# A forward Fourier transform in quarters instead of halves, an earlier table for the square root, and a new order of work, in a routed attention and gated long convolution on one core

## The chip, the cores and the metric

The kernel runs on one core of one Trainium2 chip. The metric is device time in microseconds (us) of one execution. The engines are TensorE (PE, its weight loads PEld), VectorE (DVE), ScalarE (ACT), GpSimd (POOL) and SyncE (SP), which here only issues transfers.

## What is computed

Two layers in a row, for B = 4 batches, H = 8 heads, S = 768 positions, D = 64 columns a head and 16 clusters; the model width is H x D = 512:

```
q_assign = argmax(q_n @ c_n.T);  k_assign = argmax(k_n @ c_n.T)        # nearest centroid of each q and k
scores = where(q_assign == k_assign, q @ k.T / 8, -1e9)
x = softmax(scores) @ v                                                 # [4, 768, 512]
x1, x2, x3 = split(x @ w_proj, 3)
x2_conv = irfft(rfft(x2, axis=1) * rfft(filter_fft, axis=0), axis=1)    # circular convolution along the positions
out = (x1 * x2_conv * x3) @ w_out
```

## The kernel before

**Stages.** Eight groups of four heads (n = 0 to 7, two a batch), each in two pairs of heads (pr). `routing(n)` transposes q and k on PE, compares them with the centroids, takes the arg max on DVE, and puts the result as 16 extra rows into the operands of the scores (`aug`), so that the mask comes out of the score matmul itself. `attention(n, pr)` does the scores of 128 keys at a time (line 658, by `product`), the exponential on ScalarE into `p` (667, 670), p times v on PE in float32 (681), and the sums of p on DVE (695, tile `acc`); the denominators go through transfers that fold `acc` (729, issued by POOL) and come back as `rb`; line 775 divides and stores `xT`. Every second group `hyena(b)` follows for the batch that is complete, woven into the attention of the next ones; the last batch's stands alone at the end.

**hyena(b).** U (line 807) computes x2 in six matmul groups of 64 + 64 positions. A DFT over 768 positions is done in halves: position t and its mirror image are added and subtracted (820, tile `uv2`), so that even and odd frequencies each need a sum over 384 terms, three tiles of 128 (m = 0 to 2). `spectrum(ps, i, cs)` (444) multiplies with the cosine (cs = 0) and sine (cs = 1) tables `fw`: for i = 0, 1 three steps each, for i = 2 (the 128 frequencies left over, half even, half odd) three pairs. A step of `product` is one matmul over all 128 rows or two side by side over 64 each (lines 71 and 73). The spectra are multiplied with the filter's (831, tile `tm`; `hm` holds the filter's spectrum) and combined into `y` (835). Then for each quarter dt of the channels: G projects x1 and x3 (861; copied at 868, multiplied at 871), I is the inverse transform (already in four parts, 878), 896 and 906 fold its parts into positions (`yy`), 909 forms `y2`, and W (919) multiplies by w_out; 929 copies and 936 stores the result.

**Setup.** `centroids` (306) loads and normalises the centroids: a square root on ScalarE (314), whose function table is loaded just before it, then six small DVE operations (`newton`, 316), a transpose on PE (325). `angles` (336) forms the tables `fw` in three rounds m of four DVE operations and two sines. `tables` (374) makes the inverse's tables from `fw` by transposes (392, 395), and the filter's spectrum: four loads of 384 KB, a sum and a difference on DVE (417), the same `spectrum`, and hm (437).

**The order.** Nothing runs in the order of the source. Each `op` gives its engines with a planned duration, a due time, what it reads and writes and which PSUM banks it takes; `Plan.place` (112) simulates the engines, always takes the ready operation with the earliest due time, chooses the engine where several are allowed, and yields the order in which all instructions are issued. Every engine then works through its instructions in that order and waits at each for what it needs. The due times come from T0, TAU1, TAU2 (247), from w0 and w1 of `hyena` (786), and from NUDGE (40), a list of corrections by number of operation. `lock=True` marks DVE and POOL operations that the plan does not let overlap. The first q and k loads (`load_qk`, 290) may go to SP or ACT; POOL issues the folding transfers in its own order.

Of the kernel before, what the change touches and what calls it, by code (L numbers as in the profile page):

```python
# [35 lines left out]
LEAD = 1.97516  # L36
FIRST = 2
BUSY = 8.32578
HELD = 4
NUDGE = {10:3.7,75:-1.5,90:7.4,91:7.4,129:-0.8,140:0.4,156:6.6,187:-5.6,193:0.1,212:-0.2,216:15.5,218:8.0,222:-3.8,243:1.1,253:-4.1,255:-7.1,256:-7.1,257:-3.0,264:4.3,274:2.3,281:0.9,288:9.1,289:11.6,328:-9.2,363:0.5,370:2.2,378:0.5,379:0.7,400:-0.2,406:1.5,409:-4.8,434:0.6,440:-3.7,479:0.8,480:-0.3,481:-1.3,494:-0.6,495:-4.2,508:-1.9,511:-0.2,518:-5.0,524:0.5,526:2.1,539:-2.3,554:10.5,568:1.6,573:0.4,587:-4.9,590:0.2,597:-2.4,617:0.7,620:-1.0,658:0.8,664:0.1,684:2.2,690:-8.8,740:1.0,759:0.5,767:0.4,779:-0.7,782:1.7,788:0.7,790:0.8,826:-0.5,828:-0.3,848:-2.2,872:-1.3,883:-5.3,888:-3.6,897:-0.8,898:-1.1,901:-3.5,915:-3.1,941:0.4,947:-0.4,969:-0.8,996:2.0,997:2.0,1026:2.7,1029:-2.1,1039:2.0,1043:-1.2,1048:1.2,1056:10.8,1062:0.4,1066:0.9,1098:-1.0,1101:0.3,1118:-2.2,1127:1.5,1130:-1.5,1143:-2.6,1194:-0.9,1255:0.7,1257:0.7,1263:0.3,1270:-0.2,1271:-1.1,1276:-3.6,1295:4.9,1317:-2.0,1321:0.4,1351:5.6,1373:-1.5,1441:9.4,1450:3.5,1461:2.0,1478:-1.3,1501:-8.3,1546:0.2,1557:0.1,1563:-0.6,1624:2.8,1630:-1.5,1634:0.3,1640:-4.0,1641:-4.0,1642:-13.7,1643:-4.0,1655:-4.1,1666:0.5,1685:-2.9,1771:-3.3,1776:0.2,1788:-7.8,1797:0.1,1808:-0.1,1809:-0.1,1827:-0.7,1841:-1.3,1844:0.9,1862:-0.4,1863:2.1,1887:2.4,1890:3.2,1898:-7.4,1901:-0.8,1902:-1.5,1903:-0.8,1904:-0.8,1905:-1.8,1906:-1.8}  # L40
# [27 lines left out]
def product(T, out, lhsT, rhs, start, stop):  # L68

    if T.whole:  # L70
        return T.nc.tensor.matmul(out, lhsT, rhs, start=start, stop=stop)  # L71
    for i in range(2):
        T.nc.tensor.matmul(out[64 * i:64 * i + 64], lhsT[:, 64 * i:64 * i + 64], rhs, start=start, stop=stop)  # L73


class Plan:
# [35 lines left out]
    def place(self, free0, banks_for, switch=0.1, wait=0.1, rate=215e3, bonus=11.03330, margin=0.02203, shape=1.60501):  # L112
# [130 lines left out]
def build(T):  # L243
# [3 lines left out]
    T0 = 20.36576  # L247
    TAU1 = 2.98452
    TAU2 = 3.43320
# [56 lines left out]
    def centroids():  # L306
# [3 lines left out]
        V = lambda: T.nc.vector  # L310
        op(("DVE", .23), lambda e: V().tensor_tensor(cen.c2, cen.c, cen.c, op=Alu.mult), 2.1, r=["c"], w=["c2"])
        op(("DVE", .22), lambda e: V().tensor_reduce(cen.ss, cen.c2, axis=AX, op=Alu.add), 2.2, r=["c2"], w=["ss"])
        op(("DVE", .15), lambda e: V().tensor_scalar(cen.ss, cen.ss, 1e-30, None, op0=Alu.max), 2.3, r=["ss"], w=["ss"])
        sq = op(("ACT", 1.5), lambda e: T.nc.scalar.activation(cen.s0, cen.ss, Act.Sqrt), 2.4, r=["ss"], w=["s0"])
# [21 lines left out]
    def angles(sq):  # L336
# [3 lines left out]
        for m in range(3):  # L340
            lo = 256 * (m // 2)
            n, r = (lambda x=x, m=m, lo=lo: x()[m % 2][:, :, lo:lo + 192] for x in (lambda: T.tm, lambda: T.ob))
            nk, rk = ("tm", m % 2, "a", m), ("ob", m % 2, "a", m)
# [13 lines left out]
            sins.append(op(("ACT", .52), lambda e, m=m, n=n: A_()(T.fw[:, :, m, 192:], n(), Act.Sin, scale=sc),  # L357
# [7 lines left out]
        op(("POOL", .2), one, 14, w=[("fw", m, 0) for m in range(3)])  # L365
# [8 lines left out]
    def tables(got):  # L374

        FW = [("fw", m, cs) for m in range(3) for cs in range(2)]
        fv = lambda: T.filt.rearrange("(w p m e) d -> w e p m d", w=2, p=64, m=3, e=2)
        for w_ in range(2):
            for e_ in range(2):
                op(("SP", .7), lambda e, w_=w_, e_=e_: T.nc.sync.dma_start(  # L380
                    T.f[w_][64 * e_:64 * e_ + 64], fv()[w_, e_]), 16.0, w=[("f", w_, e_)], byts=393e3, kind="load", after=got)
        for j in range(6):
            h = Bank("head")
            due = 20.0 + 2 * j

            def tr(e, j=j, h=h):
                tp = ap(h).bitcast(BF16)
                for m in range(3):
                    cols = (0, 192, 0, 192, 128, 320)[j]
                    o = tp[:, m * 128:(m + 1) * 128]  # L390
                    if j < 4:
                        T.nc.tensor.transpose(o, T.fw[:, j // 2, m, cols:cols + 128], T.identb)
                    else:
                        for i in range(2):
                            T.nc.tensor.transpose(o[64 * i:64 * i + 64], T.fw[:, i, m, cols:cols + 64], T.identb)
            op(("PE", .3 if j < 4 else .5), tr, due, r=FW + ["identb"], w=[h], alloc=h)
            half = lambda h, lo, hi: ap(h).bitcast(BF16)[lo:hi, :HS].rearrange("p (m c) -> p m c", c=64)[:, :, :32]
            if j < 4:
                op({"ACT": .35, "DVE": .3}, lambda e, j=j, h=h: copy(e, T.inv[:, j // 2, j % 2, 0], half(h, 0, 128)),
                   due + 1, r=[h], w=[("inv", j)], free=[h])  # L400
            else:
                for i in range(2):
                    op({"ACT": .35, "DVE": .3}, lambda e, i=i, j=j, h=h: copy(
                        e, T.inv[64 * i:64 * i + 64, i, j % 2, 1], half(h, 64 * i, 64 * i + 64)),
                       due + 1, r=[h, "inv0"], w=[("inv", j, i)], free=[h])
# [8 lines left out]
        F = [("f", a, b) for a in range(2) for b in range(2)]  # L414
        U2 = [("uv2", e, m) for e in range(2) for m in range(3)]
        for s_, o_ in ((0, Alu.add), (1, Alu.subtract)):
            op(("DVE", 1.75), lambda e, s_=s_, o_=o_: T.nc.vector.tensor_tensor(
                T.uv2[:, s_], T.f[0], T.f[1], op=o_), 30, r=F, w=U2[3 * s_:3 * s_ + 3], lock=True)
        for i in range(3):
            hs = [Bank("head"), Bank("head")]  # L420
            due = 34 + 4.0 * i
            for cs in range(2):
                op(("PE", .648), lambda e, i=i, cs=cs, h=hs[cs]: spectrum(ap(h), i, cs), due + 2 * cs, r=U2 + FW, w=[hs[cs]],
# [19 lines left out]

    def spectrum(ps, i, cs):
        for m in range(3):
            if i < 2:
                columns(ps, T.fw[:, i, m, 192 * cs:192 * cs + 128], T.uv2[:, i, m], m == 0, m == 2)
            else:
                for e in range(2):
                    T.nc.tensor.matmul(ps[64 * e:64 * e + 64], T.fw[:, e, m, 192 * cs + 128:192 * cs + 192],  # L450
                                       T.uv2[:, e, m], start=(m == 0), stop=(m == 2))
# [84 lines left out]
    def routing(n):  # L536
# [5 lines left out]
        for u in range(8):  # L542
# [7 lines left out]
            if n > 1 and ch == 0:  # L550
# [6 lines left out]
                for c in range(2):  # L557
                    op(EV384, lambda e, z=z, c=c, h=h: copy(e, T.qkT[z][:, c], bank(h.ids[c])[:, :384]), due + .9,
                       r=[h], w=[("qkT", z, c)], free=[h])
            elif n < 2:  # L560
# [6 lines left out]
                op(EV384 if n != 1 else {"ACT": .48}, lambda e, z=z, ch=ch, h=h: copy(e, T.qkT[z][:, ch], ap(h)[:, :384]),  # L567
# [10 lines left out]
        b0 = end - 24.00965  # L578
# [204 lines left out]
    def hyena(b):  # L783
        xs = b % 2
        last = b == B - 1
        w0 = A(24 * (b + 1)) + 11.85069
        w1 = A(24 * (b + 2)) + 50.52404 if b < B - 2 else A(96) + 34.73131
        if last:
            w0 = A(96) - 8.47659
# [8 lines left out]
        for m in range(3):  # L798
            for w_ in range(2):
# [374 lines left out]
```

The softmax here doesn't subtract the row's maximum and nothing guards it: scores larger than these inputs give would overflow.

## Time and profile before

| What | Value |
|---|---|
| median of 13 runs | 390.32 us (389.12 to 391.87) |
| the profiled execution's own time | 391.21 us |
| its span in the profile | 389.4 us |
| granted TensorE clock | 1.00 |
| MATMUL records that use uv2 and fw | 165: 15 over all rows, 150 in halves |
| DMA | 47.17 MB, mean 121 GB/s |

The page of the profile gives the busy time of each engine, the chain of waits that ended last, and groups of instructions by line: busy time and mean of one, then the idle time of the engine just before them and what ended it. A line number is one of the kernel, often of a helper: 71 and 73 are all products of PE, 260 and 262 all copies. The times of single instructions, counted from the span's start, come from the timeline; a stretch's busy times from the windows.

### The profile page before, as it was taken

What the parts mean: (1) busy time and instruction counts of PE and PEld (TensorE: products, weight loads), DVE (VectorE), ACT (ScalarE), POOL (GpSimd) and SP (SyncE); (2) the same over time, 40 slices, a digit from 0 to 9 for tenths busy, and PEclk for the clock granted to TensorE, in tenths of its full rate; (3) what the DMA queues carried; (4) which work ended last, traced back from release to release, by engine and by line L of the source; (5) the groups of instructions that cost most, each with busy time, mean ns of one, the idle gap of its engine ahead of it and who ended that gap; (6) DMA issues with size and microseconds to landing.
All of it is one profiled execution on the core that took longest, in us unless ns stands there. A gap on an engine that the chain in (4) does not pass through costs nothing.

```text
span 389.4 us, 8482 instructions
## 1 busy us (share of the span) xinstructions
PE 369.3 (95%) x3256; PEld 214.6 (55%) x3256; DVE 359.2 (92%) x509; ACT 269.9 (69%) x514; POOL 46.7 (12%) x92
## 2 busy tenths in 40 slices
PE   2999998999999999999999999999999999999995
PEld 1564454444455555555455554655454566558893
DVE  8898998898899999999899999999999999999782
ACT  5898687887884878787865976778865567632342
POOL 8502000000020011001010100101010100000400
PEclk9999999999999999999999999999999999999999
DMA  9819973740679759866997696855645651110214
GB/s 177 204 48 211 215 166 89 164 113 18 165 143 144 144 94 153 114 142 77 165 136 195 74 259 114 136 89 66 131 65 171 76 161 12 43 43 2 90 76 162
DMA packets 93860, 47.17 MB, mean 121 GB/s; under 512 B 82088, under 2 KB 87676, under 8 KB 93820
## 3 DMA queue, kind: packets, MB, share of 16 engines
q1 hardware_dynamic: 87836, 36.84, 41.5%
q0 software_dynamic: 2704, 8.98, 16.4%
q10 hardware_dynamic: 3280, 0.82, 1.1%
q8 instruction: 25, 0.41, 0.4%
q14 instruction: 15, 0.12, 0.1%
HBM read 31.59 MB, written 7.40 MB: 100 GB/s over the span
## 4 chain that ended last, share of the span: by engine, by line
PE 47%; DVE 34%; issue 8%; DMA 5%; ACT 3%; SPq 2%; DVEq 0%; POOL 0%; POOLq 0%; ACTq 0%
PE bank L73 18%; DVE acc L695 13%; PE pair L681 13%; PE bank L807 5%; DMA rb<-dr 4%; PE bank L71 3%; PE bank L555 2%; DVE oh L607 2%; DVE tm L831 2%; DVE aug L262 2%; PE bank L584 1%; DVE x L871 1%; DVE xT L775 1%; DVE mx L605 1%; PE bank L450 1%
## 5 line engine op out<-in xcount | busy, mean ns | idle before, releaser
L681 PE MATMUL pair<-p,vraw 128*64 128x385 f32 x768 | 142.9, 490 | 0.0
L670 ACT ACTIVATE p<-bank 128x512 f32<-128x512 f32 x192 | 113.5, 609 | 35.4 <-PE bank L73 33.2
L695 DVE TENSOR_TENSOR acc<-p,acc 128x1536 f32<-128x1536 f32 x64 | 112.0, 1750 | 3.5 <-ACT p L670 1.3
L681 PEld LDWEIGHTS pair<-p,vraw 128*64 128x64 f32 x768 | 54.1, 136 | 49.8 <-issue 45.2
L73 PE MATMUL bank<-aug,aug 80*64 80x512 bf16 (+3 forms) x590 | 69.7, 327 | 3.3 <-DVE den L717 1.1
L667 ACT ACTIVATE p<-bank 128x512 f32<-128x512 f32 x96 | 58.4, 608 | 3.1 <-PE bank L73 2.0
L73 PEld LDWEIGHTS <-aug 80*64 80x64 bf16 (+1 forms) x590 | 35.0, 109 | 34.7 <-issue 22.7
L729 POOL DMA_DIRECT2D acc<-acc x30 | 23.6, 788 | 246.3 <-DVE acc L695 86.5
L73 PE MATMUL bank<-xT,wpj 128*64 128x384 bf16 x424 | 41.4, 326 | 0.0
L260 ACT COPY qkT<-bank 128x384 f32<-128x384 f32 x62 | 27.9, 495 | 13.7 <-PE bank L73 8.9
L73 PEld LDWEIGHTS <-wpj 128*64 128x64 bf16 x424 | 28.0, 109 | 12.5 <-issue 6.7
L73 PEld LDWEIGHTS <-y 128*64 128x64 bf16 x448 | 25.0, 110 | 8.9 <-issue 2.9
L695 DVE TENSOR_TENSOR acc<-p,p 128x1536 f32<-128x1536 f32 x16 | 28.0, 1751 | 2.0 <-ACT p L670 2.0
L831 DVE TENSOR_TENSOR tm<-bank,hm 128x512 f32<-128x512 f32 x44 | 27.6, 678 | 0.8 <-ACT p L670 0.4
L260 ACT CAST aug<-qkT 64x768 bf16<-64x768 f32 x29 | 24.0, 830 | 3.0 <-PE bank L73 2.6
L807 PE MATMUL bank<-wpj,xT 128*64 128x512 bf16 x192 | 21.9, 380 | 0.5 <-DVE xT L775 0.5
L73 PE MATMUL bank<-wout,y 128*64 128x512 bf16 x176 | 21.4, 379 | 0.2 <-DVE y L909 0.2
L71 PE MATMUL bank<-aug,aug 80*128 80x256 bf16 (+3 forms) x89 | 20.0, 321 | 0.8 <-DVE tm L831 0.4
L555 PE MATMUL bank<-ident,qkraw 128*128 128x128 f32 x144 | 19.8, 279 | 0.2 <-DVE oh L607 0.2
L555 PEld LDWEIGHTS bank<-ident,qkraw 128*128 128x128 f32 x144 | 15.6, 140 | 7.2 <-issue 5.3
L260 ACT COPY tm<-bank 128x512 f32<-128x512 f32 x14 | 8.1, 590 | 16.2 <-PE bank L807 11.7
L262 DVE CAST aug<-qkT 64x768 bf16<-64x768 f32 x31 | 17.5, 569 | 1.5 <-PE bank L73 0.9
(149 smaller groups left out, 440.7 us busy)
## 6 DMA issues: line engine op xcount, KB each, us to landing
vraw<-in_v_dram SPq DMA_DIRECT2D x16, 384.0 KB, 3.8
qkraw<-in_q_dram SPq DMA_DIRECT2D x30, 192.0 KB, 5.1
qkraw<-in_k_dram SPq DMA_DIRECT2D x30, 192.0 KB, 4.7
rb<-dr SPq DMA_DIRECT2D x30, 192.0 KB, 3.7
out_dram<-ob SPq DMA_DIRECT2D x11, 512.0 KB, 3.8
acc<-acc POOLq DMA_DIRECT2D x10, 384.0 KB, 4.8
acc<-acc POOLq DMA_DIRECT2D x10, 192.0 KB, 3.9
y<-in_moe_filter_fft_dram SPq DMA_DIRECT2D x4, 384.0 KB, 7.7
```

The source lines that it names most:

```text
L71: return T.nc.tensor.matmul(out, lhsT, rhs, start=start, stop=stop)
L73: T.nc.tensor.matmul(out[64 * i:64 * i + 64], lhsT[:, 64 * i:64 * i + 64], rhs, start=start, stop=stop)
L260: T.nc.scalar.copy(out, in_)
L262: (T.nc.vector if e == "DVE" else T.nc.gpsimd).tensor_copy(out, in_)
L555: T.nc.tensor.transpose(bank(h.ids[i // 3])[:, ts(i % 3, 128)], raw(s, i), T.ident)
L667: T.nc.scalar.activation(o, ap(h).rearrange("p (a b) -> p a b", a=2), Act.Exp, scale=0.125)
L670: T.nc.scalar.activation(flat(s)[:, lo:lo + 512], ap(h), Act.Exp, scale=0.125)
L681: T.nc.tensor.matmul(o[64 * hp:64 * hp + 64, ch, :385], T.vraw[vs][:, hp, sk * D:(sk + 1) * D], T.p[slots[sk]][:, hp, 384 * ch:384 * ch + ...
L695: T.nc.vector.tensor_tensor(T.acc[os], P_(t[0]), P_(t[1]) if len(t) == 2 else T.acc[os], op=Alu.add)
L729: op(("POOL", .8), lambda e, rows=rows: T.nc.gpsimd.dma_start(flat_()[:rows], flat_()[rows:2 * rows], accum_op=Alu.add), te, r=[], w=[("ac ...
L807: T.nc.tensor.matmul(ap(h)[64 * i:64 * i + 64], T.xT[xs][:, kt, c:c + 64], T.wpj[:, kt, DM:2 * DM], start=kt == 0, stop=kt == ND - 1)
L831: op(("DVE", .68), lambda e, i=i, cs=cs, r=r, h=h: T.nc.vector.tensor_tensor(T.tm[r][:, cs], ap(h), hmrow(i, (0, 2, 2, 3)[2 * r + cs]), op ...
```

## The change

It has six parts.

1. *Forward transform in quarters.* The sums and differences are folded once more: x2 comes in another order of its blocks of 64 (the second half of the positions mirrored within each 64), four groups give sums and differences in `tm` as float32, `quarters` adds and subtracts those (two DVE operations over 1024 columns), the last two groups go to `uv2` directly. `spectrum` then has two steps where it had three. To have the positions mirrored, the copies of q's second half (line 558) and x1 and x3's (868, 871) read or write with a negative step, and 906 folds in blocks of 64.
2. *The filter's transform* follows: its loads become twelve of 128 KB, four float32 sums and differences, three float32 matmuls with a mirrored identity (`flip`), six more sums. `fw` has two rounds of angles instead of three, its transposes are fewer and smaller.
3. *The square root's table.* A square root on a constant (`warm`, set by DVE) is due ahead of ScalarE's first q and k issues; in the resulting order ScalarE issues the centroids, loads the table, computes the constant, then issues three of the eight first loads. SP issues the other five: both halves of the first q, and the first halves of the rest.
4. *Engines.* In batches 0 to 2 the products y (835) and y2 (909) may go to POOL; in the resulting order 22 products y are on POOL (4 before) and 2 on DVE (20 before), 10 products y2 on POOL (none before). ScalarE has 38 copies of `aug` (29 before), DVE 24 (31).
5. *The last batch* stores `y2` in the other `xT`, and its projections no longer wait for each other or for the inverse. In the resulting order eight of its groups G stand between U and the spectra, eight between the spectra and the remaining W of the batch before, and none between the inverse parts.
6. *The planner's numbers* are all new: LEAD, BUSY, NUDGE (some 400 entries instead of 150), T0, TAU1, TAU2, w0, w1, the start of the arg max, and three weights of the choice on PE.

The core of the diff:

```diff
@@ build @@
-    T0 = 20.36576
-    TAU1 = 2.98452
-    TAU2 = 3.43320
+    T0 = 16.39606
+    TAU1 = 2.39343
+    TAU2 = 3.91344
@@ centroids @@
+        op(("DVE", .1), lambda e: V().memset(T.warm, 1.0), -3, w=["warm"])
+        op(("ACT", 1.5), lambda e: T.nc.scalar.activation(T.warm, T.warm, Act.Sqrt), -2, r=[], w=["warm"])
-        sq = op(("ACT", 1.5), lambda e: T.nc.scalar.activation(cen.s0, cen.ss, Act.Sqrt), 2.4, r=["ss"], w=["s0"])
+        sq = op(("ACT", .25), lambda e: T.nc.scalar.activation(cen.s0, cen.ss, Act.Sqrt), 2.4, r=["ss", "warm"], w=["s0"])
@@ tables @@
+        f = lambda x, i: T.f[x][:, i]
+        for x in (1, 0):
+            for s_, o_ in ((1, Alu.subtract), (0, Alu.add)):
+                op(("DVE", .68), lambda e, x=x, s_=s_, o_=o_: T.nc.vector.tensor_tensor(T.tm[x][:, s_], f(x, 0), f(x, 1), op=o_),
+                   29 + x, r=F[3 * x] + F[3 * x + 1], w=[("tm", x, s_), ("tm", x)], lock=True)
+        for s_ in range(3):
+            h = Bank("head")
+            op(("PE", .9), lambda e, s_=s_, h=h: T.nc.tensor.matmul(ap(h), T.flip, f(1, 2) if s_ == 2 else T.tm[1][:, s_], start=True,
+                                                                   stop=True),
+               31 + s_, r=["flip"] + ([("tm", 1, s_)] if s_ < 2 else F[5]), w=[h], alloc=h)
@@ spectrum @@
+    def quarters(due):
+        for o_, out in ((Alu.add, slice(0, 4, 3)), (Alu.subtract, slice(1, 3))):
+            op(("DVE", 1.2), lambda e, o_=o_, out=out: T.nc.vector.tensor_tensor(T.uv2[:, out], T.tm[0], T.tm[1], op=o_), due,
...
     def spectrum(ps, i, cs):
-        for m in range(3):
+        for m in range(2):
+            slot = lambda e: T.uv2[:, 4 + (e + cs) % 2 if m else 2 * e + cs]
             if i < 2:
-                columns(ps, T.fw[:, i, m, 192 * cs:192 * cs + 128], T.uv2[:, i, m], m == 0, m == 2)
+                columns(ps, T.fw[:, i, m, 192 * cs:192 * cs + 128], slot(i), m == 0, m == 1)
@@ hyena @@
+        for u, bs in enumerate([(0, 2), (1, 3), (10, 8), (11, 9), (4, 5), (6, 7)]):
...
+            if u % 2 == 0:
+                op(EV512, lambda e, x=x, h=h: copy(e, T.tm[x][:, 0], ap(h)), due + 1, r=[h], w=k0, free=[h])
+            else:
+                for o_, i in ((Alu.subtract, 1), (Alu.add, 0)):
+                    out, w = (lambda x=x, i=i: T.tm[x][:, i], [k0, k1][i]) if u < 4 else (lambda i=i: T.uv2[:, 4 + i], [("uv2", 4 + i)])
...
+            if u == 3:
+                quarters(due + 1.5)
...
-                op({"POOL": 1.45, "DVE": .68} if last and i < 2 else ("DVE", .68), lambda e, i=i, r=r: alu(e).tensor_tensor(
+                op({"POOL": 1.45, "DVE": .68} if last and i < 2 or not last else ("DVE", .68), lambda e, i=i, r=r: alu(e).tensor_tensor(
...
-                           after=gs[-1:] + (inv[dt - 2:dt - 1] if dt > 1 else []))
+                           after=[] if last else gs[-1:] + (inv[dt - 2:dt - 1] if dt > 1 else []))
...
-            op(("DVE", .95), lambda e, dt=dt, x3=x3, yy=yy: alu(e).tensor_tensor(
-                T.y2[:, dt], yy().rearrange("p t c -> p (t c)"), x3().rearrange("p a b -> p (a b)"),
+            op({"DVE": .95, "POOL": 2.2} if not last else ("DVE", .95), lambda e, dt=dt, x3=x3, yy=yy: alu(e).tensor_tensor(
+                y2()[:, dt], yy().rearrange("p t c -> p (t c)"), x3().rearrange("p a b -> p (a b)"),
```

## The prediction

> **What bounds the kernel now.** I read the busy times and the chain of waits first, then the windows by stage, then the groups by form, last the timelines of the start and of the end.
>
> ```profile
> PE 369.3 (95%) x3256; PEld 214.6 (55%) x3256; DVE 359.2 (92%) x509; ACT 269.9 (69%) x514; POOL 46.7 (12%) x92
> ...
> PE 47%; DVE 34%; issue 8%; DMA 5%; ACT 3%; SPq 2%; DVEq 0%; POOL 0%; POOLq 0%; ACTq 0%
> ```
> Two engines are nearly full, and the chain changes between them. Which of them leads by stage:
> ```profile
> 0.00:20.00 20.00, 12.18 (x79) 7.49 (x81) 17.27 (x41) 14.04 (x27) 14.45 (x52) 1.00 0.92 196
> 40.00:110.00 70.00, 66.85 (x520) 33.45 (x518) 63.34 (x72) 56.15 (x107) 0.87 (x1) 1.00 0.58 132
> 110.00:350.00 240.00, 235.51 (x2065) 133.17 (x2063) 231.33 (x323) 169.96 (x323) 23.59 (x31) 1.00 0.63 118
> 350.00:389.40 39.40, 34.97 (x436) 29.78 (x430) 28.89 (x50) 12.90 (x25) 5.01 (x4) 1.00 0.21 81
> ```
> Columns after the stretch: PE, PEld, DVE, ACT, POOL busy. From 40 to 350 us PE idles 70 - 66.85 + 240 - 235.51 = 7.6 us and DVE 15.3 us. A busy PE is not one at its peak, so I counted its work from 120 to 340 us by the pitch of each kind (a 512-column bf16 step 0.216, a step of p times v 1.29, and so on): 212 of 220 us. PE is the bound there, DVE close behind it. After 360 us PE has no gap until 385. The start is another matter: a chain through DVE.
> ```profile
> 4.34 1.28 ACT L314 ACT_TABLE_LOAD   x1 [4.34 <-issue]
> 4.35 1.60 DVE L347 TENSOR_SCALAR ob<-x,s1t 128x384 f32<-128x384 f32 x2
> 5.64 0.20 ACT L314 ACTIVATE s<-ss 128x1 f32<-128x1 f32 x1
> 5.88 1.96 DVE L349 TENSOR_SCALAR ob<-ob 128x384 f32<-128x384 f32 x2
> 8.28 0.15 DVE L317 RECIPROCAL s<-s 128x1 f32<-128x1 f32 x1
> 10.21 0.42 PE L325 MATMUL bank<-ident,sd 128*64 128x128 f32 x1 [1.97 <-DVE sd L322]
> 12.48 2.48 PE L476 MATMUL bank<-qkT,cbd 128*32 128x384 f32 x8
> ```
> The square root's table waits for ScalarE's five DMA issues; DVE then has six angle operations in hand, so the centroids' norm begins only at 8.28, and PE, served in order, stands at L325 until 10.21.
>
> **What the Trainium skill says.** "SBUF — State Buffer", section "Who interferes with whom": a VectorE instruction with two SBUF inputs and a GpSimd instruction that reads SBUF exclude each other, and the later one blocks for the whole of the earlier. The trace has no such pair: its four y products on POOL (359.86 to 365.05) meet only VectorE operations with a PSUM input, which keep their 0.55 to 0.68 us. It has the cousin: L349 took 0.35 us alone and 1.96 for two beside POOL's memsets. "ScalarE: Activation LUTs", "What ACT_TABLE_LOAD costs": 1283 ns, and 1380 of drain. The load is 1.28 here; the drain isn't seen (5.64 follows 4.34 + 1.28). "TensorE: Matmul & The Clock Gate", "Back-to-back issue gap": 512 columns take about 216 ns; the trace agrees (below).
>
> **The change, part by part.** Counts come from both programs' orders, durations from these rows:
> ```profile
> 356.76 2.82 PE L73 MATMUL bank<-uv,fw 128*64 128x512 bf16 x24
> 359.35 0.88 PE L73 MATMUL bank<-xT,wpj 128*64 128x384 bf16 x8
> ...
> L831 DVE TENSOR_TENSOR tm<-bank,hm 128x512 f32<-128x512 f32 x44 | 27.6, 678 | 0.8 <-ACT p L670 0.4 <-POOL y L835 0.3
> L820 DVE TENSOR_TENSOR uv<-tm,bank 128x512 bf16<-128x512 f32 x24 | 15.0, 682 | 1.6 <-PE bank L807 1.6
> L835 DVE TENSOR_TENSOR y<-tm 128x512 bf16<-128x512 f32 x20 | 13.0, 678 | 0.0
> L909 DVE TENSOR_TENSOR y<-yy,x 128x768 bf16<-128x768 f32 x12 | 11.5, 958 | 0.5
> L835 POOL TENSOR_TENSOR y<-tm 128x512 bf16<-128x512 f32 x4 | 5.0, 1272 | 50.0 <-DVE tm L831 50.0
> ```
> *PE, spectra.* 24 matmuls in pairs start at 356.76, the next group at 359.35: 2.59/12 = 0.216 us a step. The filter and four batches have 90 steps; three terms become two, 60. 30 x 0.216 = **6.5 us less**. Some 24 steps lie in the crowded stages, 6 (1.3 us) in the last batch's tail, where PE has no gap either: all count.
>
> *PE, filter.* Three f32 matmuls by the flip matrix are new. No row has the shape. A step of p times v is two f32 passes of 385 columns in 1.29 us, 1.67 ns a column; x 512 = 0.86 each, **2.6 us more**, in PE's order among the first heads' scores, thus on the path (bounds 0.7 at bf16's pace, 3.0). Transposes of fw: 24 become 16, some in gaps; 0.4 less. PE in sum: **-4.3 us**.
>
> *DVE.* Two y products instead of 20: -18 x 0.678 = -12.2. Two y2 instead of 12: -10 x 0.958 = -9.6. New quarter sums, two a batch over 1024 columns: from 0.958 at 768 and 1.750 at 1536, 1.22 each, x 8 = +9.8; the stores before them replace those to uv2 (24 x 0.68 both times). Filter: two of 1.755 become four and six of 0.68, +3.3. Third angle set: -2.7. Seven aug casts go to ACT (0.569 each): -4.0. Copies, eps adds, the flip: +1.0. Sum **-14.4**, 359.2 to about 345. ACT gets nine aug casts (0.83) and loses smaller copies: +5.6 on an engine 69% busy, hidden by its idle. Mirrored copies and products: the fold L906 writes reversed in 555 ns where L896 takes 547 forward, so nothing; bound 0 to 0.1 us on some 50 operations.
>
> *POOL.* 18 products at 1.272 = 22.9, and ten y2. For these "GPSIMD Engine Reference", "3.1 Elementwise", prices two inputs at 2.6 cycles an element; scaled to the row above, an estimate of 1.8 us each: 18. They queue in order with the 30 folding DMAs of acc, two of three of which wait for the one before (78.4 us of such waits). Cost if nothing collides 0; if all collide, 22.9 + 18 = 41 us of DVE. I take a fifth, 8 us: DVE, at 353, still under today's 359. Later y delays only the inverse; heads' scores and projections fill PE meanwhile. For 1.5 us of PE's 7.6 idle I expect relief from the freer DVE (bounds -6 and +6, the re-nudged order included).
>
> *Start.* The table loads right after the centroids' issue (about 1.2 to 2.5 us), unless the memset of warm is late. ACT issues three of eight first loads instead of four, after it; SP takes one more: first k's second half is issued some 0.85 us later, v0 and v1 close behind. Data is the limit there (k at 7.36 in a stretch at 180 GB/s), so 0 to 0.8 us lost. Square root at about 4.7, behind ACT's last issue; norm 1.9 us, now ahead of the second angles; PE's L325 at 7 instead of 10.2; second angles and cbd to 9.2; similarities at about 9.3 instead of 12.48: -3.2. Late next is ACT: the exp table (1.28 + 0.20), hidden at 15.53 now, sits between the two copies of the similarities, +0.9. Net **-2.3** (bounds 0 and -4). SP has twelve filter issues instead of four, 8 x 0.65 = 5.2 us more. The mask transpose of n = 1 now stands behind eleven of them but ahead of the next q and k, behind which it left at 50.31 (those issues alone stood up to 6.6 us each); I take nothing, and the 5.2 if that cover is gone.
>
> *Tail.* After the last inverse DVE needs 8 x 0.55 + 4 x 0.96 = 8 us against PE's 5.2 + 1.7 us of W left as filler, since the projections that fill it now come earlier. About 0.5 us of wait is added; all y also wait for the quarters, with eight projections (5.2 us) as cover; without it 2.4.
>
> **Sum.** -4.3 - 2.3 - 1.5 + 0.5 = -7.6. The profiled execution took 391.21 (span 389.4 and 1.8 around it): 383.6. It lies 0.9 over the median of 13, so the median goes from 390.32 to **382.7**.
>
> **Rivals.** *DVE was the true bound* (34% of the chain; DVE 96% busy from 110 to 350): then 14 us off it also frees PE's idle and the waits inside its busy time; another 5.5 us, **377**. Against it: 212 of 220 us of PE work counted. *The new order eats the gain*: engines are served in order, every due time is new, and PE's idle grows by 5 us at masks, rb or spectra: **388**. For it: today's order leaves only 3% idle, hard to match. *POOL blocks DVE* (the other side): 28 POOL products, 41 us, against VectorE's acc (140 us), x, folds and casts, over half its time, all with two SBUF inputs. From 14.4 us of blocking (35%) DVE is as full as before; at 60%, 25 us, it is the bound with 10 more, less 2.3 at the start, and y's delay adds to it: **397**. Against it: the planner's lock keeps such pairs apart in the plan. That the change does not do what it says is excluded by the counts.
>
> **Numbers.** Forecast 0.62; DVE the bound 0.14; gain eaten 0.11 (0.07 still faster, 0.04 within 0.2%); POOL blocks 0.13. So faster 0.83, same 0.04, slower 0.13, where 0.2% (0.8 us) is what a measurement of this kernel can tell. Range 376.5 to 388.5: from the DVE case to the eaten gain, the unknown costs within; the POOL case is left out.
>
> **What would show it.** Spectra: 112 uv matmuls in pairs and four whole, PE busy near 364. Start: similarities at 9 to 10 us. DVE busy near 345 and L695 still 1750 ns: no blocking; a longer mean for acc or y2 on POOL over 2.5 us: blocking. PE gaps from 40 to 350 over 10 us: the order. The forecast is wrong if DVE's busy time does not fall, or if the similarities start after 12 us.

## The result, and the profile after

| | median | ratio to before, 95% interval |
|---|---|---|
| before, beside these runs | 390.1 us (388.81 to 392.6) | 1 |
| after | 396.09 us (393.03 to 397.65) | 1.0138 [1.0119, 1.0157] |

The change costs 1.4%, 5.4 us, where 7.6 us of gain were forecast. From here on, a difference between two kernels is the difference of their ratios to the kernel before, times 390 us; its error comes from the two intervals (root of the sum of squares). A ratio leaves out executions over 1.5% above the fastest of the same kernel: one or two of 14 to 22 in e1, e3, e6 and e12, but two of six in e8, so that e8's ratio rests on four.

The page's busy times and shares of the chain, after:

```profile
PE 369.2 (94%) x3240; PEld 209.9 (53%) x3240; DVE 356.3 (90%) x489; ACT 274.5 (70%) x521; POOL 93.3 (24%) x118
...
PE 54%; DVE 25%; DMA 8%; issue 7%; ACT 3%; SPq 2%; POOL 1%; DVEq 0%; POOLq 0%; ACTq 0%
```
PE has 16 matmuls fewer and is exactly as busy as before (369.3): work has gone, and what is left took longer. DVE fell by 3 us, not by 14. DMA's share of the chain rose from 5 to 8%. The stretches, as in the prediction (busy times of PE, PEld, DVE, ACT, POOL, then PE's clock, DMA share, GB/s):

```profile
0.00:20.00 20.00, 13.37 (x101) 8.41 (x101) 17.45 (x45) 15.43 (x31) 13.30 (x50) 1.00 1.03 199
40.00:110.00 70.00, 65.12 (x465) 31.04 (x463) 60.45 (x68) 51.31 (x98) 0.00 (x0) 0.95 0.58 129
110.00:350.00 240.00, 231.90 (x2041) 134.91 (x2039) 225.64 (x293) 174.01 (x330) 69.78 (x57) 0.99 0.61 118
350.00:394.30 44.30, 39.23 (x495) 25.09 (x491) 34.74 (x57) 15.37 (x30) 6.83 (x5) 0.99 0.18 72
```
From 40 to 350 us PE idles 70 - 65.12 + 240 - 231.90 = 13.0 us, before 7.6. And from 40 to 110 it starts 465 matmuls where it started 520, at a mean clock of 0.95. Something stopped it there. The chain of waits of that stretch, in order of time (start, length, what), names it:

```profile
37.19 1.30 DVE tm L430 x2
38.49 0.16 SPq L661
38.65 0.05 issue
38.70 10.01 DMA y<-in_moe_filter_fft_dram
48.71 0.14 issue
48.84 2.04 PE bank L434 x2
```
One transfer of 10 us lies on the path: a load of the filter. SP's timeline shows where it was issued:

```profile
25.97 7.00 SPq L390 DMA_DIRECT2D y<-in_moe_filter_fft_dram  x11
37.30 1.35 SPq L661 DMA_TRANSPOSE ohT<-oh  x1
38.70 0.58 SPq L390 DMA_DIRECT2D y<-in_moe_filter_fft_dram  x1
```
Eleven of the twelve filter loads went out from 25.97 to 32.97. The twelfth stands behind the mask transpose of n = 1 (L661), which waits for DVE's `oh` until 37.30. On POOL meanwhile, and then on PE and ACT:

```profile
32.68 0.19 POOL L1039 CAST wpj<-y 1x4 bf16<-1x4 f32 x1 [17.54 <-DMA y<-in_moe_filter_fft_dram]
33.19 2.42 POOL L1042 DMA_DIRECT2D wpj<-in_moe_w_proj_dram  x4 [0.32 <-POOL wpj L1039]
35.55 0.83 POOL L1045 DMA_DIRECT2D wout<-in_moe_w_out_dram  x1
```
```profile
42.46 1.98 PE L434 MATMUL bank<-tm,xT 128*128 128x512 f32 x4
48.84 2.04 PE L434 MATMUL bank<-y,xT 128*128 128x512 f32 x2 [4.39 <-DMA y<-in_moe_filter_fft_dram]
```
```profile
51.41 0.60 ACT L701 ACTIVATE p<-bank 128x512 f32<-128x512 f32 x1 [9.05 <-PE bank L72]
```
A copy of four elements (L1039) is to hold the weights' loads back until the filter has landed, but it reads the region of an earlier one, the seventh; so the weights' 2 MB (four loads of 384 KB, one of 512, as they land in bf16; 4 MB as they are read in float32) go out from 33.19, ahead of the twelfth filter load. Filter loads landed in 3.1 us at the median; this one took 10.01. PE works in order: the third product with the flip matrix waits for that load, and with it all scores queued behind it. ACT stands 9.05 us. When PE starts again, its clock is down (same columns as above):

```profile
48.00:50.00 2.00, 1.16 (x2) 0.65 (x3) 0.00 (x0) 0.00 (x0) 0.00 (x0) 0.58 1.31 220
50.00:52.00 2.00, 2.00 (x9) 0.49 (x10) 1.08 (x2) 0.59 (x2) 0.00 (x0) 0.50 1.20 293
52.00:54.00 2.00, 2.00 (x14) 0.40 (x8) 2.00 (x3) 0.99 (x3) 0.00 (x0) 0.50 0.55 110
54.00:56.00 2.00, 2.00 (x16) 0.97 (x14) 0.47 (x1) 1.62 (x3) 0.00 (x0) 0.71 0.27 69
```
PE reads as fully busy here, at half speed. That is one reason why its busy time did not fall.

The second difference is spread over the whole run (groups by form: busy, mean ns of one, idle before and what ended it):

```profile
L729 DVE TENSOR_TENSOR acc<-p,acc 128x1536 f32<-128x1536 f32 x64 | 116.3, 1818 | 3.9 <-ACT p L704 1.1 <-ACT p L701 0.7
L871 POOL TENSOR_TENSOR y<-tm 128x512 bf16<-128x512 f32 x22 | 30.2, 1384 | 38.7 <-DVE tm L867 37.1 <-PE bank L74 1.6
L946 POOL TENSOR_TENSOR y<-yy,x 128x768 bf16<-128x768 f32 x10 | 23.3, 2328 | 23.4 <-DVE yy L943 16.1 <-ACT x L267 5.5 <-ACT p L704 1.9
L469 DVE TENSOR_TENSOR uv<-tm,tm 128x1024 bf16<-128x1024 f32 x8 | 9.5, 1222 | 0.1
L774 DVE TENSOR_SCALAR dn<-dn 128x12 f32<-128x12 f32 x10 | 5.3, 528 | 0.3
```
The same two operations before:

```profile
L695 DVE TENSOR_TENSOR acc<-p,acc 128x1536 f32<-128x1536 f32 x64 | 112.0, 1750 | 3.5 <-ACT p L670 1.3
L740 DVE TENSOR_SCALAR dn<-dn 128x12 f32<-128x12 f32 x10 | 1.8, 177 | 0.3
```
`acc` took 1750 ns each, now 1818; the small L774 (L740 before) took 177, now 528. One place shows how:

```profile
162.20 1.50 POOL L871 TENSOR_TENSOR y<-tm 128x512 bf16<-128x512 f32 x1
162.22 1.51 DVE L774 TENSOR_SCALAR dn<-dn 128x12 f32<-128x12 f32 x1
```
```profile
164.59 1.49 PE L74 MATMUL bank<-xT,wpj 128*64 128x384 bf16 x8 [2.27 <-DVE tm L867]
```
```profile
164.00:166.00 2.00, 1.41 (x10) 1.03 (x11) 2.00 (x4) 0.00 (x0) 0.79 (x1) 0.59 0.17 39
166.00:168.00 2.00, 2.00 (x14) 1.23 (x12) 2.00 (x5) 1.39 (x3) 1.71 (x2) 0.55 0.17 61
```
DVE's 12 columns take as long as POOL's product of 512: they began 0.02 us after it. What DVE has next comes late and PE waits 2.27 us for it, of which the block explains some 1.3 (1.51 less the usual 0.18). Here too PE's clock is down afterwards: 0.59 and 0.55 as means of 2 us, 0.50 from 164.4 to 167.8 in finer stretches. From 20 to 378 us, in stretches of 2 us, these two stops are the only ones with a clock under 0.9; before has none. The blocking is what the Trainium skill states in "SBUF — State Buffer", "Who interferes with whom" ("the other fully blocks (not throttle)"). The prediction named it for operations with two SBUF inputs; the page also lists tensor_scalar, in modes that use two ports, and in this trace one is blocked.

A profile shows one execution. Over all executions of this kernel the mean granted clock lies between 0.984 and 0.995, and the time goes with it: 396.9 us at 0.984, 393.0 at 0.995. The profiled one, at 0.985, is among those that lost most.

The start went as the prediction had it:

```profile
6.30 0.88 PE L598 MATMUL bank<-ident,qkraw 128*128 128x128 f32 x3 [6.30 <-DMA qkraw<-in_q_dram]
6.97 0.42 PE L334 MATMUL bank<-ident,sd 128*64 128x128 f32 x1
9.74 1.98 PE L509 MATMUL bank<-qkT,cbd 128*32 128x384 f32 x8
```
The centroids' transpose comes at 6.97 (forecast 7, before 10.21), the similarities at 9.74 (forecast 9.3, before 12.48).

### The profile page after: what moved, and what is told of

Read it like the earlier page. It is cut to its first block, busy times and chain, and to the rows that moved or that the text cites. A ratio compares the mean times of both kernels' runs of the same rounds, so it can differ in the third digit from the quotient of the medians.

```text
span 394.3 us, 8481 instructions
## 1 busy us (share of the span) xinstructions
PE 369.2 (94%) x3240; PEld 209.9 (53%) x3240; DVE 356.3 (90%) x489; ACT 274.5 (70%) x521; POOL 93.3 (24%) x118
## 4 chain that ended last, share of the span: by engine, by line
PE 54%; DVE 25%; DMA 8%; issue 7%; ACT 3%; SPq 2%; POOL 1%; DVEq 0%; POOLq 0%; ACTq 0%
PE bank L74 19%; PE pair L715 18%; DVE acc L729 7%; PE bank L72 4%; PE bank L588 3%; DMA y<-in_moe_filter_fft_dram 3%; PE bank L841 2%; DMA ohT<-oh 2%; PE bank L618 2%; DVE oh L641 2%; DVE tm L867 2%; DMA aug<-ohT 2%; DMA qkraw<-in_k_dram 2%; PE bank L743 1%; DVE mt L652 1%
## 5 line engine op out<-in xcount | busy, mean ns | idle before, releaser
L729 DVE TENSOR_TENSOR acc<-p,acc 128x1536 f32<-128x1536 f32 x64 | 116.3, 1818 | 3.9 <-ACT p L704 1.1
L74 PE MATMUL bank<-aug,aug 128*64 128x512 bf16 (+3 forms) x588 | 67.7, 331 | 2.8 <-DMA aug<-ohT 1.3
L74 PEld LDWEIGHTS <-aug 128*64 128x64 bf16 (+1 forms) x588 | 35.8, 110 | 31.7 <-issue 22.6
L74 PE MATMUL bank<-xT,wpj 128*64 128x384 bf16 x464 | 45.3, 329 | 2.3 <-DVE tm L867 2.3
L871 POOL TENSOR_TENSOR y<-tm 128x512 bf16<-128x512 f32 x22 | 30.2, 1384 | 38.7 <-DVE tm L867 37.1
L267 ACT CAST aug<-qkT 64x768 bf16<-64x768 f32 x38 | 31.1, 830 | 0.7
L946 POOL TENSOR_TENSOR y<-yy,x 128x768 bf16<-128x768 f32 x10 | 23.3, 2328 | 23.4 <-DVE yy L943 16.1
L74 PEld LDWEIGHTS <-y 128*64 128x64 bf16 x432 | 21.3, 110 | 10.2 <-issue 3.6
L841 PE MATMUL bank<-wpj,xT 128*64 128x512 bf16 x192 | 23.4, 380 | 0.6 <-DVE xT L809 0.6
L267 ACT COPY ob<-bank 128x512 f32<-128x512 f32 x21 | 12.2, 587 | 11.4 <-PE bank L74 10.0
```

What stands on the lines that cost most here:

```text
L267: T.nc.scalar.copy(out, in_)
L729: T.nc.vector.tensor_tensor(T.acc[os], P_(t[0]), P_(t[1]) if len(t) == 2 else T.acc[os], op=Alu.add)
L841: T.nc.tensor.matmul(ap(h)[64 * i:64 * i + 64], T.xT[xs][:, kt, 64 * bs[i]:64 * bs[i] + 64], T.wpj[:, kt, DM:2 * DM], start=kt == 0, stop= ...
L871: op({"POOL": 1.45, "DVE": .68} if last and i < 2 or not last else ("DVE", .68), lambda e, i=i, r=r: alu(e).tensor_tensor(T.y[:, i, r], T. ...
```

## The experiments

**Theory.** Two losses lie on top of a small gain: PE's stop at the twelfth filter load with the slow clock after it, and DVE blocked by POOL. **Rivals.** POOL's blocking explains the whole loss, and the stop only moves work. Or the load of work on DVE and PE is what counts, and the prediction took the wrong one of them for the bound.

### The stop

**e1: the changed kernel with one transfer moved.**

```diff
     _, order = build(T)
+    last = [o for o in order if o.byts == 131e3][-1]
+    order.remove(last)
+    order.insert(next(i for i, o in enumerate(order) if o.lat == 1.0 and o.byts == 196e3), last)
```


> The kernel after, with one transfer moved: the twelfth load of the filter is issued right behind the eleventh, ahead of the mask transpose of n = 1, and nothing else is changed. Theory 1 (the late filter load stops PE, served in order, and its clock falls after the stop): 4.4 us of PE's wait at the flip matmul go, and so do some 3 us of the stretch at half clock, so 6 to 9 us less than the kernel after: about 388. Theory 2 (the loss is POOL blocking DVE all through the middle): another wait takes its place, at most 2 us less: 394.

Measured: 388.57 us, ratio 0.9942 [0.992, 0.9963]; against after -7.6 us (± 1.1). SP and PE in this kernel:

```profile
26.51 7.80 SPq L390 DMA_DIRECT2D y<-in_moe_filter_fft_dram  x12
37.85 1.42 SPq L661 DMA_TRANSPOSE ohT<-oh  x1
```
```profile
43.02 1.98 PE L434 MATMUL bank<-tm,xT 128*128 128x512 f32 x4
44.84 1.02 PE L434 MATMUL bank<-y,xT 128*128 128x512 f32 x2
45.70 0.60 PE L72 MATMUL bank<-aug,aug 80*128 80x256 bf16 x3
```
All twelve are issued by 34.3, PE goes through the three flip products without a wait, the clock stays at 1.00 in every stretch of 2 us from 48 to 56, and PE's busy time falls to 365.8 with the same 3240 matmuls. The second stop, at 162, is gone as well in this execution, though nothing was done about it: L774 is blocked here too (1.52 us at 155.76, 0.03 after POOL's product began), but PE has other work queued and waits 0.73 us. So the 7.6 us need not be the price of the first stop alone. Read from the trace of after, that one is 4.39 us of waiting, and up to 2 x (0.42 + 0.50 + 0.50 + 0.29) = 3.4 us of lost clock; the second 2.27 and up to 1.7. That is 11.8 in all, more than the 7.6 measured, so part of it is made up elsewhere; how the 7.6 divide is open. The kernel is now faster than before, by 0.6%.

**e2: the load left where it was, the weights held back.** The copy that guards them reads the twelfth load's region instead.

```diff
-        op(("POOL", .1), lambda e: T.nc.gpsimd.tensor_copy(T.wpj[0:1, :, 0:1], T.f[1][0:1, 0, 0:4].unsqueeze(2)), 29,
+        op(("POOL", .1), lambda e: T.nc.gpsimd.tensor_copy(T.wpj[64:65, :, 0:1], T.f[1][64:65, 2, 0:4].unsqueeze(2)), 29,
```


> The kernel after, with the small POOL copy that holds back the weights' loads made to wait for the twelfth load of the filter instead of the seventh. The load is still issued behind the mask transpose at about 38.7 us. If its 10 us in flight come from sharing the DMA engines with 4 MB of weights, it now lands in 3 to 4 us, the stop of PE goes and the time falls by 6 to 8 us as in the run with the load moved. If the flight has another cause, it stays near 10 us and the time stays within 1 us of the kernel after.

Measured: 389.44 us, 0.9975 [0.9954, 0.9995]. The load is again issued behind the transpose, and there is no stop:

```profile
38.92 0.57 SPq L390 DMA_DIRECT2D y<-in_moe_filter_fft_dram  x1
```
```profile
44.51 1.02 PE L434 MATMUL bank<-y,xT 128*128 128x512 f32 x2
45.37 0.60 PE L72 MATMUL bank<-aug,aug 80*128 80x256 bf16 x3
```
All filter loads here landed in at most 3.4 us. So neither the late issue alone (e2) nor the early weights alone (e1) stops PE; it takes both: a late load in flight together with 2 MB. In the Trainium skill, "DMA: Bandwidth & Descriptors", "Queues, rings and completion order", says that an engine takes turns between its queues, packet by packet; 3.1 against 10.0 us agrees with that, though no run here shows the turns themselves.

### POOL's products

**e3: the changed kernel, POOL's 28 products cut to 8 columns** (the stop is still in it; the rest of y and y2 is left out, and both are zeroed once before by two memsets on POOL).

```diff
+        cut = lambda a, e: a[:, :8] if e == "POOL" and b < B - 1 else a
...
-                    T.y[:, i, r], T.tm[r][:, 0], T.tm[r][:, 1], op=...
+                    cut(T.y[:, i, r], e), cut(T.tm[r][:, 0], e), cut(T.tm[r][:, 1], e), op=...
```


> The kernel after, with the products y and y2 that POOL does in batches 0 to 2 cut to 8 columns (so the rest of those products is left out; y and y2 are zeroed once before). It takes away POOL's 18 + 10 long products and with them any blocking of DVE, while their order stays. Theory 1: DVE's inflation of some 11 us goes (acc back to 1750 ns), but most of it lies beside PE's work: 3 to 5 us less than the kernel after, about 391 to 393. Theory 2: 8 to 10 us less, about 386 to 388.

Measured: 392.02 us, 1.0042 [1.0023, 1.0061]; against after -3.7 (± 1.1). The first stop is there (4.55 us), the second isn't. After the first the clock is down for less long than in after (0.79, 0.50 and 0.86 from 48 to 54, up to 1.7 us lost where after lost up to 3.4), so part of the 3.7 can be that. `acc` is back at its old length, and DVE's busy time near what the prediction had without blocking, 345:

```profile
PE 365.3 (94%) x3240; PEld 207.3 (53%) x3240; DVE 346.7 (89%) x489; ACT 274.3 (71%) x521; POOL 60.4 (16%) x120
```
```profile
L729 DVE TENSOR_TENSOR acc<-p,acc 128x1536 f32<-128x1536 f32 x64 | 112.0, 1750 | 3.9 <-ACT p L704 1.1 <-ACT p L701 0.7
```

**e8: both, the load first and POOL's products cut.**

> The changed kernel with the twelfth filter load issued ahead of the mask transpose of n = 1, and with POOL's 28 products (y and y2 of batches 0 to 2) cut to 8 columns, so that what they feed is not the reference's; nothing is moved to another engine. Theory 1 (the stop and the blocking are separate losses): the gains seen one at a time, 7.5 and 4, add up: 384 to 386 us, DVE busy near 347, acc's mean 1750. Theory 2 (once the stop is gone, the blocking falls into idle time of DVE): 387.5 to 389, as with the load alone. If theory 1 holds, what is left against the forecast of 382.7 is work of PE or of the order, not of POOL.

Measured: 385.4 us, 0.9866 [0.9839, 0.9892]; against e1 -3.0 (± 1.3). Theory 1: the two losses add up, 10.6 against 7.6 + 3.7. This is less firm than its interval says: four executions carry it, and with the other two, 390.67 and 390.96 us, the difference to e1 would be some -1.2. Only busy times are read from its profile (acc 1751 ns), which is of the longest of the six, with a stop of its own: PE waits 2.15 us for a copy of ScalarE, and its clock is down from 226 to 230 us. Even with the four, 2.4 us are missing to the forecast's -7.6. The busy times of e1, then of e8:

```profile
PE 365.8 (95%) x3240; PEld 209.2 (54%) x3240; DVE 355.8 (92%) x489; ACT 274.6 (71%) x521; POOL 93.7 (24%) x118
PE 366.4 (94%) x3240; PEld 208.1 (53%) x3240; DVE 347.1 (89%) x489; ACT 274.7 (71%) x521; POOL 62.2 (16%) x120
```
So the blocking takes 355.8 - 347.1 = 8.7 us of DVE's busy time.

**e7, e5, e6: the products given back to DVE, the load first.** All 28, the ten y2 alone, the 18 y alone, each at its place in the order (the three edits are shown joined).

```diff
     for o in order:
+        if o.on == "POOL" and o.eng == {"DVE": .95, "POOL": 2.2}:      # e5 and e7: y2
+            o.on = "DVE"
+        if o.on == "POOL" and o.eng == {"POOL": 1.45, "DVE": .68} and o.start < 340:      # e6 and e7: y
+            o.on = "DVE"
```


> The changed kernel with the twelfth filter load issued ahead of the mask transpose, and with all 28 POOL products (y and y2 of batches 0 to 2) given back to DVE at the places that they have in the order; the result is whole. DVE gets 18 x 0.678 + 10 x 0.958 = 21.8 us of work and loses what POOL blocked (some 11). Theory 1 (the load of POOL is worth it even with its blocking): DVE busy near 367 and the time 390 to 395. Theory 2 (the blocking and POOL's lateness cost as much as the work saves): 386 to 388.5, no slower than with the load alone, acc's mean back at 1750.

> The changed kernel with the twelfth filter load ahead of the mask transpose, and POOL's ten y2 products given back to DVE at the same places in the order; the 18 y products stay on POOL. DVE gets 10 x 0.958 = 9.6 us and loses what y2 blocked. Theory 1 (each product that leaves DVE is worth it, also when it blocks): slower than with the load alone by its share of the 6.3 us that both cost, 2.5 to 4: 391 to 393. Theory 2 (y2, at 1.8 to 3.2 us each on POOL, is the kind that blocks and comes late; y is the kind that pays): 386.5 to 389, acc's mean back near 1770.

> The changed kernel with the twelfth filter load ahead of the mask transpose, and POOL's 18 y products of batches 0 to 2 given back to DVE at the same places in the order; the ten y2 stay on POOL. DVE gets 18 x 0.678 = 12.2 us and loses what y blocked. Theory 1: slower than with the load alone by 2.5 to 4, 391 to 393. Theory 2 (y2 is the kind that does the harm): worse than the run with y2 on DVE by 3 us or more, 392 to 395, with acc's mean still near 1800.

| | ratio to before | against e1 | DVE busy (e1: 355.8) | acc, ns |
|---|---|---|---|---|
| e7, both | 1.0129 [1.0101, 1.0157] | +7.3 (± 1.4) | 365.4 | 1751 |
| e5, y2 | 0.9984 [0.9956, 1.0013] | +1.6 (± 1.4) | 358.6 | 1778 |
| e6, y | 1.0033 [1.0011, 1.0055] | +3.5 (± 1.2) | 362.3 | 1787 |

In e7, as in e8, `acc` and L774 are back at their old lengths (1751 ns in both, 174 and 173), so 365.4 - 347.1 = 18.3 us is what the 28 products add to DVE's busy time; their durations sum to 21.8, but neighbouring operations overlap. On POOL they save those 18.3 and cost 8.7 of blocking. By the lengthening of DVE's other groups against e8, each count times the difference of the means, e1 has 9.2 us of blocking, e5 (y alone on POOL) 3.7, e6 (y2 alone) 5.1: some 0.2 us a y and 0.5 a y2. What a product on POOL relieves DVE of, net, is 0.36 us for a y (6.5 us for 18) and 0.28 for a y2 (2.8 for ten). My second theory, that POOL's work is a net loss, is wrong for both kinds together; for y2 alone the gain is barely outside the error, and under the 2.5 to 4 of the first theory. A limit of these runs: the order was planned with the products on POOL, DVE now stands at their places in it, and e7's profile has a stop of PE too, 2.09 us up to 226.2, behind a copy of ScalarE.

### What bounds the kernel

Two cuts in the kernel *before*, alone and together. e4 leaves out the third of the spectra's terms (30 steps, 6.5 us of PE), e9 cuts y and y2 of batches 0 to 2 to 8 columns on DVE (zeroed before, as in e3), e10 does both.

```diff
-        for m in range(3):
+        for m in range(2):          # e4 and e10, in spectrum, stop with m == 1
...
+        cut = lambda a: a[:, :8] if b < B - 1 else a      # e9 and e10, on y, y2 and their inputs
```


> The kernel before, in its own order, with the third of the three terms of every spectrum left out (so a third of each transform's sum is missing). It removes the 30 steps of 0.216 us from PE and nothing else. If PE is the bound as the prediction took it, 6 us less than before: 384. If DVE is the true bound, 1 to 3 us less: 387 to 389.

> The kernel before, with DVE's y and y2 products of batches 0 to 2 cut to 8 columns, so that what they feed is not the reference's: some 20 us less DVE work, the same order and the same work on PE. Theory 1 (DVE is what PE waits for; the work that left PE in the run with two terms became idle time because DVE did not finish sooner): 5 to 9 us faster, 381 to 385. Theory 2 (PE's own work is the bound, as the prediction had it): at most its idle time behind DVE, 1 to 3 us, 387.5 to 389.5. Theory 3 (neither engine but the written order with its transfers and ScalarE): within 1 us of before.

> The kernel before with both cuts: the third spectrum term left out (6.5 us of PE) and y and y2 of batches 0 to 2 cut to 8 columns (20 us of DVE); what they feed is not the reference's. Theory 1 (PE and DVE are both bounds, stage by stage, so that PE's 6.5 us count only where DVE is relieved too): 4 to 6 us under the run with DVE's cut alone, 376 to 380. Theory 2 (PE's work is the bound throughout): some 5 us under DVE's cut alone too, but from 388: 383. Theory 3 (the written order, its transfers and ScalarE): within 2 us of either cut alone.

| | work taken out | median | ratio | gain |
|---|---|---|---|---|
| e4 | PE 6.5 | 389.53 | 0.9969 [0.9951, 0.9987] | 1.2 us |
| e9 | DVE 18 | 387.56 | 0.9943 [0.9923, 0.9964] | 2.2 us |
| e10 | both | 384.76 | 0.9858 [0.9836, 0.988] | 5.5 us |

The busy times of before (in the prediction) against those of e4, then e10:

```profile
PE 363.7 (93%) x3201; PEld 210.5 (54%) x3201; DVE 358.8 (92%) x509; ACT 270.1 (69%) x514; POOL 46.8 (12%) x92
```
```profile
PE 361.3 (94%) x3201; PEld 203.7 (53%) x3201; DVE 341.5 (89%) x509; ACT 269.4 (70%) x514; POOL 52.6 (14%) x94
```
In e4 PE lost 5.6 us of busy time, and nearly all of it turned into idle time: span less busy was 389.4 - 369.3 = 20.1 and is 389.1 - 363.7 = 25.4, of which 310 - (65.91 + 231.30) = 12.8 us lie between 40 and 350, against 7.6 before:

```profile
40.00:110.00 70.00, 65.91 (x510) 32.83 (x508) 63.47 (x73) 56.06 (x107) 0.63 (x1) 1.00 0.55 126
110.00:350.00 240.00, 231.30 (x2020) 130.20 (x2018) 230.26 (x320) 170.36 (x324) 23.89 (x31) 1.00 0.67 120
```
DVE, at 230.26 of 240, is as full as it was (231.33). Together the cuts give more than the sum of both, 5.5 against 3.4 (the 2.1 between them ± 1.4, with four executions of e10): the same 6.5 us of PE are worth 1.2 us alone and 3.3 (± 1.2) where DVE is relieved too. That is theory 1 in kind: both engines bound the kernel, in turn. Its sizes were too high: I had expected 5 to 9 us from DVE's cut alone, and 376 to 380 us with both. By number e9's 2.2 and e10's 384.76 lie nearer to theory 2, PE's work alone (1 to 3, and 383); against that speaks e4, where 6.5 us off PE gave 1.2. Some 25 us of work give 5.5 us; the rest stays in the written order, in which each engine waits for the others' results. Which of those waits they are was not taken apart.

### The start

**e11 and e12: the changed kernel with the load first, and the start partly undone.** e11 leaves out the early square root (and the memset of `warm`); e12 also puts DVE's second set of angles ahead of the centroids' norm (the two edits are shown joined).

```diff
     _, order = build(T)
+    second = [[o for o in order if line(o) == k][1] for k in (355, 357, 359, 362)]      # e12
+    order = [o for o in order if o not in second]
+    at = next(i for i, o in enumerate(order) if line(o) == 325)
+    order[at:at] = second
+    order = [o for o in order if line(o) not in (318, 319)]      # e11 and e12
```


> The changed kernel with the twelfth filter load ahead of the mask transpose, and without the early square root: the memset of warm and the first square root are left out, so that the table loads after ScalarE's DMA issues as in the kernel before; the result is whole. Theory 1 (the start is on the path and its gain is carried to the end): the centroids' norm comes 1.2 to 1.5 us later, the similarities at 10.8 to 11.3 instead of 9.7, and the time is 1 to 1.5 us more than with the load alone: 389.6 to 390.1. Theory 2 (the early gain is used up at the next handover, in the masks or in DVE's queue): within 0.5 us of the load alone, 388 to 389.

> The changed kernel with the twelfth filter load ahead of the mask transpose, and with the start put back to the order of before as far as it goes: no early square root, and DVE's second angle set ahead of the centroids' norm; the result is whole. Theory 1 (the prediction's step: the similarities' start is what the stage gains or loses): with the norm some 2.2 us later, the similarities come at 11.5 to 12, and the time is 2 to 2.3 us more than with the load alone, 390.6 to 390.9. Theory 2 (PE has transposes to do while the norm is late, so only its idle time counts; up to the first head's end that was 8.0 us in the kernel before and 6.6 with the load alone): 0.7 to 1.5 more, 389.3 to 390.1. Theory 3 (the early gain does not last to the end at all): within 0.5 of the load alone.

Measured: e11 388.85 us, 0.9932 [0.9906, 0.9958], against e1 -0.4 (± 1.3); e12 389.68 us, 0.9986 [0.996, 1.0012], against e1 +1.7 (± 1.3). In e11 the similarities came at 9.91 instead of 9.61; in e12:

```profile
8.74 0.42 PE L334 MATMUL bank<-ident,sd 128*64 128x128 f32 x1 [1.55 <-DVE sd L331]
...
11.01 2.41 PE L509 MATMUL bank<-qkT,cbd 128*32 128x384 f32 x8
```
The early table itself is worth nothing that can be measured: the norm began at 4.51 with it and at 4.71 without, since ScalarE issues one transfer less ahead of it than before, and even the late load of the table ends at 4.47. What counts is DVE's order, the norm ahead of the second angles: 1.4 us at the similarities (9.61 in e1, 11.01 in e12), and 1.55 us of PE's idle time. The 1.7 at the end lies nearest to theory 2 (0.7 to 1.5); theory 1's 2 to 2.3 is within its error.

## Why the prediction was wrong

From the forecast of -7.6 to the measured +5.4 it is 13.0 us. Three of its steps failed. The runs give 7.6 (e1) and 3.0 (e8) for the first two; 2.4 is what remains, put down to the third without a run of its own.

**1. SP's twelve filter issues: "I take nothing, and the 5.2 if that cover is gone".** This is the largest failure. The step counted the eight added issues and asked who stands *behind* them; it even noted that the transpose of n = 1 stands behind *eleven*. It did not ask where the twelfth stands, nor who waits for it. It stands behind an instruction that waits for DVE; its reader is a PE instruction with all scores behind it; and between issue and reader the weights start on another queue. The flip products were priced by their durations ("2.6 us more ... thus on the path") and never asked when their input would land. Moving the load gave 7.6 (e1), keeping the weights away 6.4 (e2). Wait and clock are both in that, and whatever the second stop cost, which neither kernel's profile has: in after the two passes of the third product took 1124 ns each at the mean, in e2 592.

**2. POOL's collisions: "I take a fifth, 8 us: DVE, at 353, still under today's 359", at no cost.** The size was right: 8.7 us (9.2 by durations), a fifth of POOL's 18 x 1.384 + 10 x 2.328 = 48 us. A y2 took 2.33 us on average where 1.8 was estimated (its shortest 1.81), and DVE stands at 356 for 353, since its own work fell by 12.1 (e8) and not by 14.4. The failed part is the conclusion that what stays under 359 costs nothing: without the blocking the kernel gains another 3.0 us (e8) to 3.7 (e3), with the doubts named there. A wait inside DVE comes at one place and is handed on there, as at 162.22; a sum over the whole run doesn't show it. The rival "POOL blocks DVE" forecast 397 (its own terms, 390.3 + 10 - 2.3, make 398 before any delay of y). That is close to what came, by luck: its blocking stayed under the 14.4 us from which it was to decide, and POOL's work was a gain on balance (e7).

**3. PE "is the bound there, DVE close behind it"; the steps "all count".** 212 of 220 us of PE work were counted, but DVE was at 231 of 240 from 110 to 350, and with both engines over 95% full the work that PE lost was found again as its idle time (e4). 6.5 us were worth 1.2 alone, 3.3 with DVE relieved. The rival "DVE was the true bound" fails the same way: 18 us off DVE gave 2.2. And the relief expected "for 1.5 us of PE's 7.6 idle" turned round: with the load first PE idles 70 - 67.88 + 240 - 233.06 = 9.1 us from 40 to 350. The rival "the new order eats the gain" was nearer than its 388 shows: PE's idle in that stretch was to grow by 5 and grew by 5.4, to 13.0, past the 10 us named as its sign. But it was to come at masks, rb or spectra, not at the filter's load, and the slow clock was not in it.

**What held.** *Spectra*: 112 matmuls in pairs and four whole, as counted. *The start*: similarities at 9.74 for 9.3, although PE's first transposes came 1.2 us later than before (6.30 for 5.12), past the 0.8 allowed for; the gain of 2.3 measured 1.7 (± 1.3), with its cause in DVE's order rather than in the table. *Quarter sums*: 1222 ns for 1.22. *DVE's count*: 346.7 without blocking for 345. *Flip products*: in e1 they follow each other at 0.91 and 0.86 us, for 0.86. *Tail*: idle time after 350 us was 4.4 before and is 37 - 31.92 = 5.1 in e1, for +0.5. *PE's sum*: -3.5 in e1 for -4.3. One small term of it had the wrong sign. The transposes of fw were to save 0.4; sixteen smaller ones, in pairs of two sizes, take 0.29 to 0.32 us a pair, some 2.4 in all, where before groups of three took 0.16 to 0.27 and two groups of six 0.36, some 1.5.

So the change with its twelfth load ahead of the transpose is a gain of 0.6% (e1), of which the start may be most (1.7 ± 1.3 of 2.3 us).

## What to carry to other kernels

Where a step adds transfers to an in-order queue, find the last one: what stands ahead of it, who reads it, and what else is in flight between issue and reader; counting issues is not enough. Where two engines are nearly full, price removed work by relieving both, since either alone may give a fraction, as here. Work moved to POOL is worth its saving less its blocking: here a shorter product (0.68 us on DVE) relieved DVE of 0.36 us net, a longer one (0.96) of 0.28. A busy time that stays under the old one is no proof that a wait inside it costs nothing.

## What the runs showed of the hardware

- After 4.39 us of idle PE ran at 0.50 of its clock until 55.2, and after 2.27 us at 0.50 from 164.4 to 167.8; in the profile of e8 2.15 us up to 225.7 were followed by 0.50 (226 to 228), but 2.31 us earlier in the same execution (56.7 to 59.1) left it at 1.00, as did 1.55 us in e12 (7.2 to 8.7). In the Trainium skill, "TensorE: Matmul & The Clock Gate", "Why this matters for your kernels", advises against idle gaps of over about 3 us; here shorter ones came ahead of a slow clock, so the measurement decides; and a gap's length alone doesn't tell.
- The slow clock cost up to 3.4 us on top of a wait of 4.39, 1.7 on 2.27, and 1.7 on 4.55 (e3). The loss shows as busy time of PE: 369.2 us in after, 365.8 in e1, for the same 3240 matmuls.
- A tensor_scalar of 12 columns took 1.51 us beside POOL's product, 177 ns on average in the kernel before: as long as POOL's product (1.50), not as its own size asks.
- A load of 128 KB, issued at 38.7, took 10.0 us behind 2 MB that POOL had issued on another queue from 33.2 on, and at most 3.4 with those 2 MB held back (e2).
